# Whole PSUM banks for the low-rank expansion from tile 80 on, with V on four row tiles

## The chip, the cores and the metric

The kernel runs on one core of a Trainium2 chip. A core has a matrix engine (TensorE, PE in the profile), VectorE (DVE), ScalarE (ACT), GpSimd (POOL) and SyncE (SP). Each takes its own instructions in order, and semaphores join them. Matmuls write to PSUM, which is cut into 8 banks of 512 fp32 columns on 128 partitions. DVE and ACT move results from there to SBUF. The metric is the device time of one execution in microseconds (us); the median of three runs is 323.24 (323.01 to 324.3).

## The reference

There are 8 batches of 4224 positions with 192 channels. First comes a short causal convolution along the positions: 7 taps, one softmaxed set of taps for each of 8 heads of 24 channels. Then comes a mixer, whose low-rank part mixes positions (U and V have rank 32), and whose second part is a two-layer network on the channels (192 to 768 to 192).

```python
x = conv(x, softmax(weight))              # (8, 4224, 192), called y in the kernel
h = x.transpose(0, 2, 1) @ U @ V          # U: 4224 x 32, V: 32 x 4224
u = x + h.transpose(0, 2, 1)
out = u + np.maximum(u @ w_ch1, 0.0) @ w_ch2
```

## The kernel before

The positions of a batch are cut into 33 tiles of 128, so that there are 264 tiles in all. Eight tiles make a group, and there are 33 groups. A batch's 33 tiles and a group's 8 don't divide each other, so a group can hold tiles of two batches.

For each batch the steps are these. `conv32` (c) makes y: eight matmuls a head (L349), written to two banks that `evac` copies to SBUF on ACT (L266) or DVE (L268). A string of letters, used in a ring, says which engine takes which copy. It reads x and a shifted copy of x, which POOL makes in six copies (`x_shift`, L303 to L315); there is one such buffer, so the shift for the next batch starts after the conv of this one. `tt_mm` (t) multiplies the 33 tiles by U (L412, four column tiles of the array at a time), `tt_split` makes a high and a low bf16 part (L426 on ACT, L427 on DVE), and `tt_sum` (s) adds the four column tiles with two matmuls (L438), so that the product of rank 32 then stands four times, on partitions 0, 32, 64 and 96; DVE copies it to SBUF (L432).

For the tiles of a batch `h_tiles` (h) expands that product by V: one matmul a tile (L469) with 32 rows, 128 output partitions and 192 columns. The four places of 32 rows in the array, here called row tiles, can work side by side. Two neighbouring tiles form a pair. A pair shares a bank (384 of the 512 columns) and a row tile, the pair's number modulo four, and V is stored in `V_sb` for each tile on that row tile alone. One DVE instruction (L492) adds y and writes a pair's u in bf16; where a pair is cut by the edge of a batch, of a half group or of the span, there are two. When a group's u is whole, SP issues a DMA transpose of it (`transp`, L513).

For each group `w1` runs 36 matmuls (L589), in pairs on two row halves, 512 columns each; a pair of banks is emptied by ACT and DVE with a relu (L603, L605). `w2` runs 12 matmuls (L616) for two tiles, DVE adds u (L625), and SP issues the DMA to the output (L633).

The schedule is written out by hand. `SLOTS` is a list of stages. From stage 5 on a stage runs w1 of three groups (108 matmuls of L589), and then 12 w2 pieces of 12 matmuls. Between the w2 pieces a table says what else PE does at which piece p (0 to 12): c, t, s, h, and x for POOL's shift. Loads of x for later batches are issued by POOL and held back until a certain matmul of w1 is done (`LOADS`). PSUM has one pool of eight banks; each `bank()` takes the next in turn, and waits until that bank's last reader is done. The h spans of the late stages are in `spans`, two or three in a stage:

```python
        5: [(80, 88), (88, 96), (96, 105)],
        6: [(105, 117), (117, 129)],
```

A `w` entry runs `h_span` over its tiles and then issues the transposes of the groups that it completes. Stage 5 begins with group 6, stage 13 with group 30; the last conv is in stage 9, the last h in stage 12.

Of the kernel before, what the change touches and what calls it, by code (L numbers as in the profile page):

```python
# [7 lines left out]
ALU = mybir.AluOpType  # L8
ACT = mybir.ActivationFunctionType
BF16 = mybir.dt.bfloat16  # L10
# [4 lines left out]
def kernel(  # L15
# [10 lines left out]
    nc = tc.nc  # L26
    P = nc.NUM_PARTITIONS
    B, S, D = x.shape
# [16 lines left out]
    cst = ctx.enter_context(tc.tile_pool(name="cst", bufs=1))  # L45
# [10 lines left out]
    def bank():  # L56
        return psp.tile([P, 512], F32, name="ps", tag="ps")
# [5 lines left out]
    yt = [None] * B  # L63
# [39 lines left out]
    def iota(t, pattern, base, mul):  # L103
# [20 lines left out]
        out=Ur[:, 0:nfull, :], in_=U4[0 : nfull * P, :].rearrange("(k p) c -> p k c", p=P)  # L124
# [29 lines left out]
    for r in range(4):  # L154
        nc.vector.memset(rq[QB * r : QB * r + QB, 0:1], float(QB * r))
    nc.vector.tensor_scalar(
        out=rq[:, 1:2], in0=rq[:, 0:1], scalar1=-4.0, scalar2=None, op0=ALU.mult
# [19 lines left out]
    for hh in range(2):  # L177
# [3 lines left out]
        out=dif[:], in0=dif[:], scalar1=rq[:, 0:1], scalar2=None, op0=ALU.add  # L181
# [5 lines left out]
        out=d_sb[:],  # L187
        in0=w_sb[:],
        in1=mx_sb[:].unsqueeze(2).to_broadcast([P, H, KC]),
        op=ALU.subtract,  # L190
# [5 lines left out]
        out=hot[:],  # L196
        in0=dif[:].unsqueeze(1).to_broadcast([P, KC, BW]),
        in1=tap[:].unsqueeze(2).to_broadcast([P, KC, BW]),
        op=ALU.is_equal,
# [3 lines left out]
        out=ident[:], in0=fp[:], scalar1=float(P), scalar2=None, op0=ALU.is_equal  # L203
# [9 lines left out]
        out=c_sb[:].rearrange("p k h -> p h k"),  # L213
        in0=e_sb[:],
        in1=rs_sb[:].unsqueeze(2).to_broadcast([P, H, KC]),
        op=ALU.mult,
    )
    prs = []
    for hh in range(2):
# [3 lines left out]
            out=pr[:],  # L223
            in0=hot[:].unsqueeze(2).to_broadcast([P, KC, HQ, BW]),
            in1=c_sb[:, :, HQ * hh : HQ * hh + HQ].unsqueeze(3).to_broadcast([P, KC, HQ, BW]),
            op=ALU.mult,
# [5 lines left out]
        out=Eq[:], in0=efp[:], scalar1=rq[:, 1:2], scalar2=None, op0=ALU.is_equal  # L232
# [3 lines left out]
        out=fp[:], in0=fp[:], scalar1=R - 1, scalar2=None, op0=ALU.bitwise_and  # L236
# [3 lines left out]
        out=R4[:], in0=fp[:], scalar1=0.0, scalar2=None, op0=ALU.is_equal  # L240
# [163 lines left out]
    ttb = [[] for _ in range(B)]  # L404
# [17 lines left out]
    def tt_split(b, p):  # L422

        hi = sml.tile([P, D], BF16, name="tt_hi")
        lo = sml.tile([P, D], BF16, name="tt_lo")
        nc.scalar.activation(out=hi[:], in_=p[:, 0:D], func=ACT.Copy)  # L426
        nc.vector.tensor_tensor(out=lo[:], in0=p[:, 0:D], in1=hi[:], op=ALU.subtract)  # L427
        ttb[b] += [hi, lo]
# [22 lines left out]
    def u_group(g):  # L451
        if ut[g] is None:
            ut[g] = us.tile([P, 4, 3, 2, HB], BF16, name="u_sb")
        return ut[g]
# [46 lines left out]
    def h_span(t0, t1):  # L501
        while t0 < t1:
            b = t0 // NT
            te = min(t1, (b + 1) * NT)
            h_tiles(b, t0 - b * NT, te - b * NT)
            t0 = te

    def h_group(g):
        h_span(g * GT, g * GT + GT)

    def transp(g):
        uTt[g] = uts.tile([P, 4, 3, P], BF16, name="uT")
        return nc.sync.dma_start_transpose(  # L513
            out=uTt[g][:].rearrange("p i c t -> p (i c) t"),
            in_=ut[g][:].rearrange("p i c f k -> p (i c f k)"),
        )
# [118 lines left out]
    def held(ins, after):  # L635
        tc.add_manual_dep(
            ins.ins,
            after.ins.name,
            mybir.DependencyInfo(mybir.DependencyClass.Sync, mybir.DependencyReason.DATA),
            reason="transfer held back",  # L640
        )

    def x_load(b, q, after):
        if q == 0:
            x_tile(b)
            x_zero(b, nc.gpsimd)
        held(x_part(b, *XP[q]), after)
# [25 lines left out]
            },  # L673
        ),
    ]
    spans = {
        5: [(80, 88), (88, 96), (96, 105)],
        6: [(105, 117), (117, 129)],
        7: [(129, 140), (140, 152)],
        8: [(152, 164), (164, 175)],  # L680
        9: [(175, 187), (187, 198)],
        10: [(198, 210), (210, 222)],
        11: [(222, 233), (233, 245)],
        12: [(245, 253), (253, 264)],
        13: [],
    }
    for k in range(5, 14):
        gs = list(range(3 * k - 9, 3 * k - 6))
        hs = [f"w{t0}:{t1}" for t0, t1 in spans[k]]
        if k == 5:  # L690
            at = {
                2: ["c3:0:3:AAD"],
                3: ["c3:3:3:AAD"],
                4: ["c3:6:2:A", "x4:4"],
                5: [hs[0]],
                6: ["t3"],
                8: ["s3", hs[1]],
                11: [hs[2]],
            }
        elif k < 10:  # L700
            b = k - 2
            at = {
                0: [f"c{b}:0:2:AAD"],
                2: [f"c{b}:2:3:A"],
                4: [f"c{b}:5:3:AD"] + ([f"x{b + 1}:4"] if b + 1 < B else []),
                5: [hs[0]],
                9: [f"t{b}", hs[1]],
                12: [f"s{b}"],
            }
        elif k < 13:  # L710
            at = {0 if k == 12 else 2: [hs[0]], 5 if k == 12 else 7: [hs[1]]}
        else:
            at = {}
        SLOTS.append((gs, gs, at))

    LOADS = {3: [(4, 1), (4, 4), (5, 1), (5, 4)]}
    for b in range(4, B):
        g = 3 * b - 6
# [26 lines left out]
    for r, (k0, k1) in KP[2].items():  # L745
        j = NB0 // 2 * r + k0
        nc.gpsimd.tensor_copy(
            out=U4_sb[:, o : o + k1 - k0, :, :],
            in_=U_sb[:]
# [8 lines left out]
        out=V_sb[0:32, 2 * (NT // 8), :], in_=moe_V[:, (NT - 1) * P : NT * P]  # L758
# [35 lines left out]
    for r in range(4):  # L794
        q = slice(QB * r, QB * r + QB)
        for hh in range(2):
            nc.gpsimd.tensor_copy(
                out=band2[q, HQ * hh : HQ * hh + HQ, :],
                in_=bands[hh][q, :, HB * (r % 2) : HB * (r % 2) + QB],
            )  # L800

    def do(what):
        if what[0] == "c":
            b, h0, n, engs = what[1:].split(":")
            conv32(int(b), int(h0), int(n), engs)
            return
        if what[0] == "d":
            for h in range(H):
                last = conv(int(what[1:]), h, 1, [0, 1], "AA" if h == 2 else "AD")
            held(transp(3), last)  # L810
            done.append(last)
            return
        if what[0] == "l":
            b, q = (int(v) for v in what[1:].split(":"))
            x_load(b, q, done[-1])
            return
        if what[0] == "x":
            b, n = (int(v) for v in what[1:].split(":"))
            if not steps:
                steps.extend(x_shift(b))  # L820
            for _ in range(n):
                steps.pop(0)()
            return
        if what[0] == "w":
            t0, t1 = (int(v) for v in what[1:].split(":"))
            h_span(t0, t1)
            for g in range(t0 // GT, t1 // GT):
                transp(g)
            return
        n = int(what[1:])  # L830
        if what[0] == "h":
            h_group(n)
            if n > 1 and n != 3:
                transp(n)
        elif what[0] == "t":
            tt_split(n, tt_mm(n, range(NT)))
        else:
            tt_sum(n)

    for gs1, gs2, at in SLOTS:  # L840
        for g in gs1:
            ends = w1(g, RELU0 if g == 1 else RELU)
            for b, blocks in LOADS.items():
                for q, (gb, m) in enumerate(blocks):
                    if gb == g:
                        x_load(b, q, ends[m])
                        if steps:
                            steps.pop(0)()
            if g == 0:
                do("h2")  # L850
        while steps and gs1 != [3]:
            steps.pop(0)()
        npc = 4 * len(gs2)
        for p in range(npc + 1):
            for what in at.get(p, []):
                do(what)
            if p < npc:
                g, k = gs2[p // 4], p % 4
                if g == NG - 1 and k == 3:
                    w2(g, 6, 1)  # L860
                    w2(g, 7, 1)
                else:
                    w2(g, 2 * k, 2)
# [30 lines left out]
```

## Time and profile before

| what | us |
|---|---|
| median of three runs | 323.24 |
| the profiled execution | 323.12 |
| its span, first to last instruction | 321.3 |
| PE busy | 314.9 (98%) |
| DVE busy | 268.7 (84%) |
| ACT busy | 169.5 (53%) |
| POOL busy | 141.6 (44%) |

The page also gives the groups that the change touches: 264 matmuls of h at L469 with 12.0 us in which at least one is under way, 168 adds at L492 with 65.8 us, and 133 adds of w2 at L625 with 69.5 us. Ten groups (80 tiles) are made before tile 80 in the old way, in both kernels.

How to read it: an engine's busy time is the time in which at least one of its instructions is under way. Matmuls overlap, so the durations of single ones add up to more than that. The chain that ended last follows the work back from the end; a stretch of it that is all PE, without gaps, means that nothing but PE's own instructions set the time there. A wait in a row of another engine costs time only if that engine's work is on this chain.

### The profile page before, as it was taken

The numbers are of one execution on the slowest core, as the hardware profiler recorded it, in microseconds if no ns is written. First come the engines' busy times: TensorE is split into PE (matmuls) and PEld (weight loads), VectorE is DVE, ScalarE is ACT, GpSimd is POOL, SyncE is SP. The second block draws the span as 40 slices with busy tenths as digits, with TensorE's granted clock in tenths as the row PEclk, the third lists the DMA queues.
The fourth block names the chain that finished last, engine by engine and source line by source line (L and its number), as shares of the span: only waits on it lengthen the run. The fifth ranks groups of instructions, "written<-read, shape, count | busy, mean of one in ns | idle before, by whom it ended". The sixth has DMA issues, their size and how long they took to land.

```text
span 321.3 us, 9597 instructions
## 1 busy us (share of the span) xinstructions
PE 314.9 (98%) x4004; PEld 218.7 (68%) x4004; DVE 268.7 (84%) x550; ACT 169.5 (53%) x344; POOL 141.6 (44%) x108
## 2 busy tenths in 40 slices
PE   7999999999999999999999999999999999999996
PEld 3757576478677647946864884686597497487495
DVE  6779989987977986996998699699898888897864
ACT  1766723960874396088249609824904903912910
POOL 8763199529947982993798398000000000000000
PEclk9999999999999999999999999999999999999999
DMA  9999993998997999799799963169077079059035
GB/s 105 191 195 169 196 232 101 196 190 253 210 165 147 263 153 194 189 201 154 191 241 139 191 185 111 52 179 218 2 215 228 3 169 275 2 171 272 2 109 188
DMA packets 122443, 53.39 MB, mean 166 GB/s; under 512 B 87712, under 2 KB 122400, under 8 KB 122400
## 3 DMA queue, kind: packets, MB, share of 16 engines
q1 hardware_dynamic: 84528, 38.08, 46.0%
q0 software_dynamic: 37728, 14.60, 39.6%
q8 instruction: 31, 0.51, 0.7%
q14 instruction: 12, 0.10, 0.1%
q10 hardware_dynamic: 144, 0.10, 0.1%
HBM read 29.22 MB, written 25.95 MB: 172 GB/s over the span
## 4 chain that ended last, share of the span: by engine, by line
PE 91%; ACT 3%; DMA 2%; DVE 2%; POOL 1%; issue 1%; POOLq 0%
PE ps L616 42%; PE ps L589 39%; PE ps L349 3%; PE ps L469 3%; DMA x_sb<-in_x_dram 2%; PE ps L412 2%; ACT rl_sb L603 2%; ACT y_sb L266 1%; PE ps L379 1%; POOL x_sb L79 1%; DVE u_sb L492 1%; DVE rl_sb L605 1%; PE ps L438 0%; PE ps L536 0%; DVE out_sb L625 0%
## 5 line engine op out<-in xcount | busy, mean ns | idle before, releaser
L603 ACT ACTIVATE rl_sb<-ps 128x512 bf16<-128x512 f32 x233 | 124.3, 604 | 89.1 <-PE ps L589 77.6
L616 PE MATMUL ps<-W_sb,rl_sb 128*128 128x192 bf16 x1584 | 139.8, 246 | 0.2
L616 PEld LDWEIGHTS <-rl_sb 128*128 128x128 bf16 x1584 | 128.4, 98 | 12.2 <-issue 11.9
L589 PE MATMUL ps<-uT,W_sb 64*128 64x512 bf16 x1188 | 131.5, 376 | 0.3 <-DVE uT L268 0.2
L605 DVE TENSOR_SCALAR rl_sb<-ps 128x512 bf16<-128x512 f32 x163 | 105.7, 688 | 15.2 <-PE ps L589 14.9
L589 PEld LDWEIGHTS <-W_sb 64*128 64x128 bf16 x1188 | 61.3, 94 | 65.9 <-issue 3.0
L625 DVE TENSOR_TENSOR out_sb<-ps,u_sb 128x384 f32<-128x384 f32 (+1 forms) x133 | 69.5, 550 | 25.9 <-PE ps L616 25.0
L315 POOL COPY xb_sb<-x_sb 32x3072 bf16<-32x3072 bf16 (+1 forms) x24 | 67.7, 2820 | 1.1
L492 DVE TENSOR_TENSOR u_sb<-y_sb,ps 128x192 bf16<-128x192 bf16 (+1 forms) x168 | 65.8, 461 | 0.0
L303 POOL COPY xb_sb<-x_sb 128x3072 bf16<-128x3072 bf16 x12 | 32.9, 2742 | 41.5 <-PE ps L349 33.8
L266 ACT ACTIVATE y_sb<-ps 128x408 bf16<-128x408 f32 (+4 forms) x90 | 38.2, 519 | 11.9 <-PE ps L349 9.8
L79 POOL DMA_DIRECT2D x_sb<-in_x_dram x32 | 27.1, 852 | 12.5 <-PE ps L469 7.7
L268 DVE CAST y_sb<-ps 128x408 bf16<-128x408 f32 (+4 forms) x36 | 19.2, 578 | 1.3 <-PE ps L379 1.2
L426 ACT ACTIVATE tt_hi<-ps 128x192 bf16<-128x192 f32 x8 | 2.6, 330 | 27.4 <-PE ps L412 27.4
L469 PE MATMUL ps<-tt_sb,V_sb 32*128 32x192 bf16 x264 | 12.0, 245 | 0.0
L349 PE MATMUL ps<-x_sb,band 64*32 64x384 bf16 x192 | 11.8, 332 | 0.0
L349 PE MATMUL ps<-xb_sb,band 64*32 64x384 bf16 x192 | 11.8, 331 | 0.0
L469 PEld LDWEIGHTS <-V_sb 32*128 32x128 bf16 x264 | 5.8, 92 | 5.7 <-issue 5.5
L379 PE MATMUL ps<-x_sb,band 64*64 64x240 bf16 (+3 forms) x192 | 8.0, 276 | 0.4 <-DMA x_sb<-in_x_dram 0.3
L379 PEld LDWEIGHTS <-band 64*64 64x64 bf16 x192 | 6.0, 106 | 2.2 <-issue 1.5
L349 PEld LDWEIGHTS <-band 64*32 64x32 bf16 x384 | 4.3, 89 | 4.7 <-issue 2.4
L412 PE MATMUL ps<-y_sb,U_sb 128*32 128x192 bf16 x258 | 7.4, 247 | 0.0
(65 smaller groups left out, 66.5 us busy)
## 6 DMA issues: line engine op xcount, KB each, us to landing
out_dram<-out_sb SPq DMA_DIRECT2D x131, 192.0 KB, 3.0
x_sb<-in_x_dram POOLq DMA_DIRECT2D x14, 384.0 KB, 7.2
x_sb<-in_x_dram POOLq DMA_DIRECT2D x7, 432.0 KB, 7.8
x_sb<-in_x_dram POOLq DMA_DIRECT2D x7, 408.0 KB, 7.2
W_sb<-in_moe_w_ch_dram POOLq DMA_DIRECT2D x3, 288.0 KB, 7.5
x_sb<-in_x_dram POOLq DMA_DIRECT2D x1, 504.0 KB, 7.4
uT<-u_sb SPq DMA_TRANSPOSE x31, 3.8
x_sb<-in_x_dram POOLq DMA_DIRECT2D x1, 480.0 KB, 5.6
```

The source lines that it names most:

```text
L79: return nc.gpsimd.dma_start(out=xt[b][HB * r : HB * r + HB, s0:s1, :], in_=x[b, blk * HB : (blk + s1 - s0) * HB, :].rearrange("(j p) d -> ...
L266: nc.scalar.activation(out=out, in_=in_, func=ACT.Copy)
L303: nc.gpsimd.tensor_copy(out=xbt[b][:, s0:s1, :], in_=xt[b][:, s0 + 1 : s1 + 1, :])
L315: nc.gpsimd.tensor_copy(out=xbt[b][q, s0:s1, :], in_=xt[b][q, s0:s1, :])
L349: nc.tensor.matmul(out=pp[r][QB * cg : QB * cg + QB, 0 : nk[r] * GS], lhsT=w[hr], rhs=t[hr, st : st + 2 * nk[r] - 1 : 2, hs], start=True, ...
L469: last = nc.tensor.matmul(out=banks[pr][:, a * D : (a + 1) * D], lhsT=V_sb[32 * q : 32 * q + 32, (j // 8) * 2 + j % 2, :], rhs=ttb[b][32 * ...
L492: nc.vector.tensor_tensor(out=u_group(g)[:, i : i + n, :, hf, :], in0=yt[b][:, run[0] : run[0] + n, :].rearrange("p n (c k) -> p n c k", c=3),
L589: last = nc.tensor.matmul(out=pps[m][hf][:], lhsT=W1_sb[HB * hf : HB * hf + HB, c, m * P : (m + 1) * P], rhs=uTt[g][HB * hf : HB * hf + HB ...
L603: nc.scalar.activation(out=rl[:, m, hf, :], in_=pp[hf][:], func=ACT.Relu)
L605: nc.vector.tensor_scalar_max(out=rl[:, m, hf, :], in0=pp[hf][:], scalar1=0.0)
L616: last = nc.tensor.matmul(out=cps[:, a * D : (a + 1) * D], lhsT=rlt[g][:, m, hf, (i + a) * P : (i + a + 1) * P], rhs=W2_sb[:, m, :], start ...
L625: nc.vector.tensor_tensor(out=o[:, 0:n, :].rearrange("p n (c k) -> p n c k", c=3), in0=cps[:, 0 : n * D].rearrange("p (n c k) -> p n c k", ...
```

## The change

From tile 80 on the columns of u are counted in units of 64 (three to a tile). A bank takes eight units, all of its 512 columns, whatever tiles they belong to; a tile that falls across two banks is done in two matmuls of 64 and 128 columns. So eight tiles fill three banks, with ten matmuls in place of eight. Each bank's matmuls stand on one row tile, and the banks of a cluster take the four row tiles in turn, four banks at a time; within such a four the first matmul of each bank is issued, then the second of each, and so on. For that, any tile may be needed on any row tile, so a second copy of V, whole on each of the four, is loaded by POOL in four DMAs after w1 of group 5 (`V4_sb`). DVE adds y for a whole bank at once, cut where a half group or a batch ends: 96 adds where there were 119.

The tiles 80 to 263 are 69 banks. They are made in 14 clusters of 4, 6 or 7 banks, in place of 17 clusters of 8 to 12 tiles. The tables of the stages 5 to 13 are rewritten, with the convs, the products by U, the sums and the shifts in new places, and with other engines for some copies of y (one copy fewer on DVE in stages 5 and 6, two more in each of 7 to 9). In the strings below, `7:b7` means a cluster of 7 banks ahead of w2 piece 7.

```diff
+    TH0 = 80
+    NCH = 3 * TH0
+    V4_sb = cst.tile([P, NT, P], BF16, name="V4_sb")
+
+    def v4_load():
+        for q in range(4):
+            nc.gpsimd.dma_start(
+                out=V4_sb[32 * q : 32 * q + 32, :, :],
+                in_=moe_V[:, :].rearrange("r (j t) -> r j t", t=P),
+            )
+
+    made = [0]
+
+    def h_banks(n):
+
+        c0 = NCH + 8 * made[0]
+        made[0] += n
+        c1 = c0 + 8 * n
+        assert c1 <= 3 * NTT
+        for s0 in range(c0, c1, 32):
+            ps, todo = [], []
+            for k in range(s0, min(s0 + 32, c1), 8):
+                p, q, parts = bank(), len(ps), []
+                for t in range(k // 3, (k + 7) // 3 + 1):
+                    a, e = max(k, 3 * t), min(k + 8, 3 * t + 3)
+                    parts.append((p, q, k, t, a, e))
+                ps.append((p, k))
+                todo.append(parts)
+            for n in range(max(len(parts) for parts in todo)):
+                for parts in todo:
+                    if n >= len(parts):
+                        continue
+                    p, q, k, t, a, e = parts[n]
+                    nc.tensor.matmul(
+                        out=p[:, HB * (a - k) : HB * (e - k)],
+                        lhsT=V4_sb[32 * q : 32 * q + 32, t % NT, :],
+                        rhs=ttb[t // NT][
+                            32 * q : 32 * q + 32, HB * (a - 3 * t) : HB * (e - 3 * t)
+                        ],
...
+            for p, k in ps:
+                a = k
+                while a < k + 8:
+                    b, blk = a // (3 * NT), a // 12
+                    e = min(k + 8, 12 * (blk + 1), 3 * NT * (b + 1))
...
+                    nc.vector.tensor_tensor(
...
+                    a = e
+        for g in range(c0 // 24, c1 // 24):
+            transp(g)
...
-    spans = {
-        5: [(80, 88), (88, 96), (96, 105)],
-        6: [(105, 117), (117, 129)],
-        7: [(129, 140), (140, 152)],
-        8: [(152, 164), (164, 175)],
-        9: [(175, 187), (187, 198)],
-        10: [(198, 210), (210, 222)],
-        11: [(222, 233), (233, 245)],
-        12: [(245, 253), (253, 264)],
-        13: [],
+    late_slots = {
+        5: "2:c3:0:3:AAD 4:c3:3:3:AAAD 5:c3:6:2:A 5:x4:4 7:b7 7:t3 12:s3",
+        6: "0:b4 2:c4:0:2:A 4:c4:2:3:AD 5:c4:5:3:A 5:x5:4 7:b7",
+        7: "0:c5:0:2:AD 0:t4 0:c5:2:3:AD 2:s4 3:c5:5:3:AAAD 3:x6:4 4:b4 7:b4",
+        8: "0:c6:0:2:AAD 1:c6:2:3:AAD 2:c6:5:3:AD 2:x7:4 2:t5 2:b4 4:s5 7:b6",
+        9: "0:c7:0:2:AD 1:c7:2:3:AAD 5:c7:5:3:AAD 6:b4 9:b4 9:t6 9:t7 12:s6 12:s7",
+        10: "0:b4 6:b6",
+        11: "0:b4 6:b7",
+        12: "0:b4",
+        13: "",
     }
...
-        if k == 5:
-            at = {
-                2: ["c3:0:3:AAD"],
-                3: ["c3:3:3:AAD"],
-                4: ["c3:6:2:A", "x4:4"],
-                5: [hs[0]],
-                6: ["t3"],
-                8: ["s3", hs[1]],
-                11: [hs[2]],
-            }
-        elif k < 10:
-            b = k - 2
-            at = {
-                0: [f"c{b}:0:2:AAD"],
-                2: [f"c{b}:2:3:A"],
-                4: [f"c{b}:5:3:AD"] + ([f"x{b + 1}:4"] if b + 1 < B else []),
-                5: [hs[0]],
-                9: [f"t{b}", hs[1]],
-                12: [f"s{b}"],
-            }
-        elif k < 13:
-            at = {0 if k == 12 else 2: [hs[0]], 5 if k == 12 else 7: [hs[1]]}
-        else:
-            at = {}
+        at = {}
+        for item in late_slots[k].split():
+            p, what = item.split(":", 1)
+            at.setdefault(int(p), []).append(what)
         SLOTS.append((gs, gs, at))
...
-        if what[0] == "w":
-            t0, t1 = (int(v) for v in what[1:].split(":"))
-            h_span(t0, t1)
-            for g in range(t0 // GT, t1 // GT):
-                transp(g)
+        if what[0] == "b":
+            h_banks(int(what[1:]))
             return
...
+            if g == 5:
+                v4_load()
```

More of the change, by code (lines that the diff above doesn't have):

```diff
@@ L506, in h_span @@
             t0 = te
+    TH0 = 80
[33 more added lines that the diff above has]
+                        ],
+                        start=True,
+                        stop=True,
+                        tile_position=(32 * q, 0),
+                    )
+            for p, k in ps:
[3 more added lines that the diff above has]
+                    e = min(k + 8, 12 * (blk + 1), 3 * NT * (b + 1))
+                    y0, i0 = a - 3 * NT * b, a - 12 * blk
+                    nc.vector.tensor_tensor(
+                        out=u_group(blk // 2)[:].rearrange("p i c f k -> p (i c) f k")[
+                            :, i0 : i0 + e - a, blk % 2, :
+                        ],
+                        in0=yt[b][:].rearrange("p j (c k) -> p (j c) k", c=3)[
+                            :, y0 : y0 + e - a, :
+                        ],
+                        in1=p[:, HB * (a - k) : HB * (e - k)].rearrange(
+                            "p (n k) -> p n k", k=HB
+                        ),
+                        op=ALU.add,
+                    )
+                    a = e
+        for g in range(c0 // 24, c1 // 24):
+            transp(g)
@@ L688 @@
         gs = list(range(3 * k - 9, 3 * k - 6))
-        hs = [f"w{t0}:{t1}" for t0, t1 in spans[k]]
-        if k == 5:
-            at = {
-                2: ["c3:0:3:AAD"],
-                3: ["c3:3:3:AAD"],
-                4: ["c3:6:2:A", "x4:4"],
-                5: [hs[0]],
-                6: ["t3"],
-                8: ["s3", hs[1]],
-                11: [hs[2]],
-            }
-        elif k < 10:
-            b = k - 2
-            at = {
-                0: [f"c{b}:0:2:AAD"],
-                2: [f"c{b}:2:3:A"],
-                4: [f"c{b}:5:3:AD"] + ([f"x{b + 1}:4"] if b + 1 < B else []),
-                5: [hs[0]],
-                9: [f"t{b}", hs[1]],
-                12: [f"s{b}"],
-            }
-        elif k < 13:
-            at = {0 if k == 12 else 2: [hs[0]], 5 if k == 12 else 7: [hs[1]]}
-        else:
-            at = {}
+        at = {}
+        for item in late_slots[k].split():
+            p, what = item.split(":", 1)
+            at.setdefault(int(p), []).append(what)
         SLOTS.append((gs, gs, at))
```

## The prediction

> **What bounds the kernel now.** I read the page's busy shares first, then the chain that ended last, then that chain in order of time, and last the timeline of single engines in one late stage.
>
> The page says that TensorE (PE) is busy nearly always, at a granted clock (PEclk) of nine tenths or more of full speed in every slice, and that the chain is made of its work:
>
> ```profile
> span 321.3 us, 9597 instructions
> ...
> PE 314.9 (98%) x4004; PEld 218.7 (68%) x4004; DVE 268.7 (84%) x550; ACT 169.5 (53%) x344; POOL 141.6 (44%) x108
> ...
> PEclk9999999999999999999999999999999999999999
> ...
> PE 91%; ACT 3%; DMA 2%; DVE 2%; POOL 1%; issue 1%; POOLq 0%
> ```
>
> Now one late stage (k = 8) of the chain in order of time; the columns are start, length, what and how many. Some matmul records are missing, so counts of L349 are low (16 and 24 were issued).
>
> ```profile
> 164.42 11.76 PE ps L589 x108
> 176.18 0.47 PE ps L349 x11
> 176.65 2.09 PE ps L616 x24
> 178.74 0.64 PE ps L349 x19
> 179.38 2.08 PE ps L616 x24
> 181.46 0.64 PE ps L349 x19
> 182.10 1.10 PE ps L616 x12
> 183.20 0.43 PE ps L469 x12
> 183.63 4.07 PE ps L616 x48
> 187.70 0.85 PE ps L412 x33
> 188.55 0.51 PE ps L469 x11
> 189.06 3.08 PE ps L616 x36
> 192.14 0.17 PE ps L438 x2
> ```
>
> Each piece starts where the one before it ends: PE is the bound from the first w1 of stage 5 (80.51 us) to the last w2 matmul (318.17), 237.66 us. Only PE's own work there, or a new wait in it, can move the end. Two prices follow. From 12 to 24 matmuls of L616 is 1.10 to 2.09, so a matmul of 192 columns takes 82.5 ns and **each run of one kind costs about 0.11 us beyond its matmuls** (L412: 9 rounds x 0.0825 + 0.11 = 0.85; L469 x12: 4 rounds + 0.10). s (L438) after w2 adds only its two matmuls and opens no run. Second, **an h cluster lasts as long as its fullest row tile**: by the code the 12 tiles at 183.20 put 2, 2, 4, 4 on the four row tiles (4 x 0.0825 = 0.33), the 11 tiles at 188.55 put 5, 2, 2, 2, and last longer. A model of pieces plus 0.11 to 0.13 a run gives 237.7 for the whole stretch, so there are no hidden waits in it to win back.
>
> **The change part by part.**
>
> *h matmuls.* Before, 17 clusters; summing the fullest row tile of each gives 63 rounds x 82.5 ns = 5.20 us. After, 69 banks in 14 clusters (nine of 4 banks, two of 6, three of 7), the k-th bank of every four on row tile k: 19 rounds of 512 columns. Matmuls go from 184 to 230: 138 of 192 columns, 46 of 128, 46 of 64. The durations of 192 columns (82.5 ns), 408 (a conv head, 0.17 us) and 512 (L589: 11.65 us over 54 pairs, 216 ns) lie on one line, 0.417 ns a column and 2.4 ns a matmul. By it 512 columns in three or four pieces take 0.22 us: 19 x 0.22 = 4.25, a **saving of 0.95**. No row shows a 64-column piece. If every piece costs a whole 82.5 ns, a four-piece bank takes 0.33 and the sum is 6.2: a loss of 1.0. If the row tiles keep step (each round as long as its longest piece), 0.267 a round, 5.05: a saving of 0.15. I take the line through the durations, as all rows lie on it, and keep both.
>
> That row tiles do not keep step the windows show, for the matmuls of L469 in the cluster at 188.48 (PE and weight loads that touch each stretch):
>
> ```profile
> 188.47:188.56 0.09, 0.08 (x4) 0.09 (x8) 1.00 1.10 294
> 188.56:188.63 0.07, 0.07 (x8) 0.07 (x9) 1.00 1.02 326
> ```
>
> Four matmuls run in the first 0.09 us, though in program order the second of them stands on the same row tile as the first and must wait 82 ns. The others passed it. The Trainium skill ("TensorE: Matmul & The Clock Gate", Part 3, "What overlaps and what doesn't") says that matmuls start and end strictly in program order; by it the sum would be the 5.05 above, and the trace disagrees with it here.
>
> *Fewer runs on PE.* Counting the runs of one kind in program order, s with w2: before 16 in stage 5, 12 in each of 6 to 9, 6, 6, 5, 2 = 83; after 11, 11, 11, 11, 12, 5, 5, 3, 2 = 71. They go because clusters are fewer, a tt or an h stands straight behind a conv or an h, and t6 and t7 stand together. 12 x 0.11 = **1.3 saved** (1.2 to 1.6 with conv's 0.13). w1, w2, conv, tt and s keep their matmuls: nothing.
>
> *PSUM banks.* A cluster of 7 takes seven of the eight; the w2 piece behind it gets the bank of the w2 just before it. That one's add starts 0.03 us after its matmuls and takes 0.56 (the L625 row), so the bank is free after 0.65, while the cluster lasts 0.11 + 0.44: a **wait of about 0.1, three times**. Behind 6 banks or 4 the next bank has been free for 1 us. All this holds if VectorE (DVE) is in step when the cluster starts, as it is before the clusters of today:
>
> ```profile
> 180.51 0.56 DVE L625 TENSOR_TENSOR out_sb<-ps,u_sb 128x384 f32<-128x384 f32 x1 [1.18 <-PE ps L616]
> 181.50 0.56 DVE L625 TENSOR_TENSOR out_sb<-ps,u_sb 128x384 f32<-128x384 f32 x1 [0.43 <-PE ps L616]
> ```
>
> *DVE.* 119 adds (65 of 384 columns, 54 of 192) become 96 (44 of 512, 44 of 256, 8 others) over the same columns; by 547 and 347 ns a fixed 147 ns is saved 23 times at most. Four more y copies (0.55 each) go from ACT to DVE. Stages 6, 8, 10 and 11 get 3 to 6 more tiles (0.25 us each by L492's 5.6 us for 23) and 7 to 9 two more copies, so at most 1.5 us on 23.7 to 24.2 busy of some 27.8 (in 10 and 11 on 22 of 24.9). All off PE's path. Behind a 7-bank cluster DVE holds some 4.4 us of adds; PE runs on, as it asks for one bank per 1.0 us and DVE frees one per 0.6 to 0.7. What is queued behind them, the w2 adds and then the first relu of w1, is under a microsecond late, and each group of w1 leaves DVE 0.6 idle (its waits in L605) to catch up.
>
> *POOL and its DMAs.* The four V loads (0.5 to 1 us to issue each, by the V_sb and x rows) fall in POOL's idle stretch before 70.66 (6.2 us, it waits there for conv). They move 1.1 MB in bf16; by queue q0's 14.6 MB for 39.6% of the span that is some 9 us of the 16 engines, first used near 99 us. Without that cover the first cluster would wait. On SP only transposes move; each group is written at least 6 us before its w1, against 3.8 us to land. In stage 6 the shift of x for batch 5 (L303 to L315) starts one w2 piece later and conv 5 opens stage 7. POOL needs 19.4 us from release to the last copy:
>
> ```profile
> 126.63 2.74 POOL L303 COPY xb_sb<-x_sb 128x3072 bf16<-128x3072 bf16 x1 [7.05 <-PE ps L349]
> ...
> 142.94 3.06 POOL L315 COPY xb_sb<-x_sb 32x3456 bf16<-32x3456 bf16 x1
> ```
>
> PE arrives after 2.09 + 0.55 + 5.06 + 11.76 = 19.5 (today 21.9). With 0.1 to start, a **wait of 0.1**, where it was covered by 2.4. The other stages keep 2 us or more.
>
> *Sum.* 0.95 + 1.3 - 0.4 = 1.85 us. The profiled execution took 323.12 (321.3 and 1.8 around the span), 0.12 below the median of 323.24; from the median: **321.4 us**.
>
> **The rivals.** A measurement of this kernel can tell 0.5% (1.6 us) from no change: the bounds are 321.6 and 324.9.
>
> 1. *Short pieces cost a whole slot.* For: 46 more matmuls, each with its own weight load, 0.09 us by the PEld row. Against: on the row tile with five tiles, pieces follow each other every 82 ns, so a load is hidden behind 80 ns of work; for 27 ns of work nothing shows it. h then costs 6.2: 323.3 us. The Trainium skill (same page and part) lets a weight load overlap only matmuls on other row groups, which is this rival's mechanism.
> 2. *Row tiles in step.* Against it stand the windows above: 322.2 us.
> 3. *DVE empties the banks too late (slower).* Everything a large cluster writes is emptied by DVE alone. If DVE is 0.7 us or more behind when such a cluster starts, the next w2 waits for that long each time, and a late bank goes on into w1. Five large clusters at 0.7 eat the gain and give 324.9; at 1.0 each, 326. For: DVE already has 85% in these stages, and more y copies in 7 to 9. Against: the idle 0.43 before its w2 adds. At the far end, all of a cluster's adds ahead of the next w2 (4.4 us), the times would be near 340, but the order of the banks excludes it.
>
> **How the numbers follow.** The forecast has 0.56 and a range of its own of 320.4 to 322.2 (no new waits and 0.13 a run; pieces at 50 ns): 0.45 below 321.6, 0.11 above. Rival 1 has 0.12, rival 2 0.10, both within 0.5%; rival 3 has 0.22. So faster 0.45, same 0.33, slower 0.22. The likeliest is 321.4; the range 320.4 to 324.9 leaves out most of rival 3 and a little below.
>
> **What would show it.** In the chain in order of time: a 4-bank cluster of 13 or 14 matmuls at 0.33 us (0.44 for rival 1, 0.38 for rival 2), a 7-bank one at 0.55; 71 runs between 80.5 us and the end. PE waiting for DVE behind the large clusters for more than 0.1 us would be rival 3; a gap before the first conv of stage 7 with POOL as its releaser is the late shift. DVE's wait rows for PE before w2 adds should shrink but not vanish. I am wrong if PE's pieces no longer follow each other without gaps, or if a run costs less where it stands behind another kind than w2.

## The result, and the profile after

| | before | after |
|---|---|---|
| median, us | 323.15 (323.01 to 324.3) | 332.64 (332.01 to 337.57) |
| the profiled execution, us | 323.12 | 332.01 |
| its span, us | 321.3 | 330.2 |

The change made the kernel slower, by a ratio of 1.0279 (1.0242 to 1.0316). The forecast was 321.4. Ratios here and below are made from undisturbed executions alone, so some are lower than the medians beside them would give.

The page of the kernel after still has PE busy nearly always, but for one dent, and there the granted clock falls too:

```profile
PE   8999999995499999999999999999999999999996
...
PEclk9999999999599999999999999999999999999999
...
PE 88%; DMA 6%; DVE 2%; ACT 2%; issue 1%; POOL 0%; DVEq 0%; POOLq 0%
```

The 40 slices are 8.3 us each; the dent is in the tenth and eleventh, 74 to 91 us. It is in stage 4, before the first of the new clusters. The chain in order of time shows what stands there (start, length, what, how many):

```profile
73.39 1.92 PE ps L681 x22
75.31 11.00 DMA out_dram<-out_sb
...
86.42 0.43 DVE u_sb L492 x2
...
87.54 0.47 PE ps L469 x5
88.02 2.06 PE ps L681 x12
90.08 12.85 PE ps L654 x108
```

The same place in the chain of the kernel before:

```profile
80.51 11.84 PE ps L589 x108
92.34 2.09 PE ps L616 x24
```

The first w1 of stage 5 (that of group 6) now begins at 90.08, 9.57 late. It takes 12.85 where it took 11.84, because the clock is still 0.50 after the pause. By the end of this w1 10.59 us are lost. From there to the last w2 matmul it is 224.11 (102.93 to 327.04) where it was 225.83 (92.34 to 318.17): **1.72 gained**. So the profiled execution is 8.9 us longer: 10.59 lost in one place, 1.72 won in the rest.

Of the 9.57, 7.5 is time in which PE does nothing, from 79.07 to 86.56. The rest is lost in the matmuls behind it, which wait for DVE to catch up and run at the lower clock: 12 matmuls of w2 take 2.06 (88.02) where they took 1.10.

The waits say who stopped whom. PE waits for DVE to make banks free (and stands before an old cluster, L469); DVE waits for an output buffer, which is free when the output from it has landed (us in all, times, the longest):

```profile
DVE out_sb L690 <- DMA out_dram<-out_sb: 9.6, 1, 9.6
...
PE ps L469 <- DVE out_sb L690: 7.5, 1, 7.5
```

The outputs are issued by SP. Its timeline before, and then after (start, duration, what):

```profile
66.67 2.50 SPq L513 DMA_TRANSPOSE uT<-u_sb  x1
69.26 8.71 SPq L633 DMA_DIRECT2D out_dram<-out_sb  x9
79.24 1.41 SPq L513 DMA_TRANSPOSE uT<-u_sb  x1
```

```profile
66.61 7.61 SPq L578 DMA_TRANSPOSE uT<-u_sb  x1
74.31 12.59 SPq L698 DMA_DIRECT2D out_dram<-out_sb  x9
88.44 1.41 SPq L578 DMA_TRANSPOSE uT<-u_sb  x1
```

A transpose whose issue took 2.50 now holds SP for 7.61. It lands after 19 us, the longest of uT's landings, which go from 7.9 to 19.0 (a landing is counted from the issue; before, then after):

```profile
DMA to landing us min/median/max: 3.2/3.8/7.9
```

```profile
DMA to landing us min/median/max: 3.2/3.5/19.0
```

The windows show the transfers at this moment (length, then PE, PEld, DVE, ACT, POOL, clock, share of the 16 DMA engines, GB/s): first before, then after.

```profile
74.00:78.00 4.00, 4.00 (x54) 3.69 (x52) 2.86 (x8) 0.00 (x0) 3.96 (x2) 1.00 1.10 366
78.00:82.00 4.00, 4.00 (x50) 2.70 (x49) 4.00 (x10) 0.66 (x2) 3.88 (x3) 1.00 0.89 176
```

```profile
74.00:78.00 4.00, 4.00 (x54) 3.69 (x53) 1.52 (x4) 0.00 (x0) 3.96 (x2) 1.00 1.33 142
78.00:82.00 4.00, 1.07 (x13) 0.93 (x12) 0.00 (x0) 0.00 (x0) 3.88 (x3) 1.00 1.31 22
```

At 78 to 82 us packets are under way on the DMA engines for more of the time than before (the share, a sum over the queues that can pass 1, is 1.31 against 0.89), and yet only 22 GB/s are moved, where it was 176. What is new among the transfers is the load of V, which POOL issues in 2.03 us right before, as forecast, and which takes 16.1 us to land:

```profile
64.38 2.03 POOL L514 DMA_DIRECT2D V_sb<-in_moe_V_dram  x4
```

```profile
V_sb<-in_moe_V_dram POOLq DMA_DIRECT2D x4, 264.0 KB, 16.1
```

The DMA queues of the kernel after from 78 to 82 us (packets, MB, share of the 16 engines' time) show why so little moves. q0 is POOL's queue, q1 SP's:

```profile
q1 hardware_dynamic: 144, 0.04, 125.1%
q0 software_dynamic: 9, 0.05, 6.1%
```

The load's queue takes 6.1% of 16 engines, which is the time of one. The packet records have one row of 8448 bytes after another there, 0.64 us each, the last of them until 82.9. In the same 4 us SP's queue starts only 144 packets of 256 bytes, and they take a median of 0.66 us where 0.02 is usual. From 83 to 87 us, with the last row gone, 347 GB/s are moved. So the end of the load, on what looks like a single engine (the records name none), held back transfers that are spread over all of them.

### The profile page after: what moved, and what is told of

The parts are those of the page before. It is cut to its first block, busy times and chain, and to the rows that moved or that the text cites. A ratio compares the mean times of both kernels' runs of the same rounds, so it can differ in the third digit from the quotient of the medians.

```text
span 330.2 us, 9677 instructions
## 1 busy us (share of the span) xinstructions
PE 316.9 (96%) x4050; PEld 218.4 (66%) x4050; DVE 269.9 (82%) x531; ACT 167.8 (51%) x340; POOL 143.6 (43%) x112
## 4 chain that ended last, share of the span: by engine, by line
PE 88%; DMA 6%; DVE 2%; ACT 2%; issue 1%; POOL 0%; DVEq 0%; POOLq 0%
PE ps L681 40%; PE ps L654 39%; DMA out_dram<-out_sb 3%; PE ps L349 3%; DMA x_sb<-in_x_dram 2%; PE ps L412 2%; PE ps L379 2%; PE ps L541 1%; ACT rl_sb L668 1%; DVE u_sb L492 1%; DVE out_sb L690 1%; PE ps L469 1%; ACT y_sb L266 1%; DVE rl_sb L670 1%; PE ps L601 0%
## 5 line engine op out<-in xcount | busy, mean ns | idle before, releaser
L681 PEld LDWEIGHTS <-rl_sb 128*128 128x128 bf16 x1584 | 129.7, 98 | 10.0 <-issue 8.2
L654 PEld LDWEIGHTS <-W_sb 64*128 64x128 bf16 x1188 | 58.8, 94 | 69.6 <-issue 4.6
L266 ACT ACTIVATE y_sb<-ps 128x384 bf16<-128x384 f32 (+4 forms) x86 | 36.4, 519 | 17.0 <-PE ps L349 15.1
L557 DVE TENSOR_TENSOR u_sb<-y_sb,ps 128x512 bf16<-128x512 bf16 (+5 forms) x96 | 44.1, 527 | 0.0
L268 DVE CAST y_sb<-ps 128x408 bf16<-128x408 f32 (+4 forms) x40 | 21.3, 577 | 1.3 <-PE ps L379 1.2
L492 DVE TENSOR_TENSOR u_sb<-y_sb,ps 128x384 bf16<-128x384 bf16 (+1 forms) x49 | 19.9, 471 | 0.0
L469 PE MATMUL ps<-tt_sb,V_sb 32*128 32x192 bf16 x80 | 4.8, 255 | 7.7 <-DVE out_sb L690 7.5
L469 PEld LDWEIGHTS <-V_sb 32*128 32x128 bf16 x80 | 1.9, 92 | 10.9 <-issue 10.9
L163 PE MATMUL ps<-zz 128*128 128x512 f32 (+1 forms) x10 | 7.2, 878 | 1.1 <-DVE zz L151 1.1
L426 ACT ACTIVATE tt_hi<-ps 128x192 bf16<-128x192 f32 x8 | 2.6, 330 | 10.2 <-PE ps L412 10.2
## 6 DMA issues: line engine op xcount, KB each, us to landing
V_sb<-in_moe_V_dram POOLq DMA_DIRECT2D x4, 264.0 KB, 16.1
```

Of the source, the lines that this page charges most:

```text
L266: nc.scalar.activation(out=out, in_=in_, func=ACT.Copy)
L492: nc.vector.tensor_tensor(out=u_group(g)[:, i : i + n, :, hf, :], in0=yt[b][:, run[0] : run[0] + n, :].rearrange("p n (c k) -> p n c k", c=3),
L557: nc.vector.tensor_tensor(out=u_group(blk // 2)[:].rearrange("p i c f k -> p (i c) f k")[:, i0 : i0 + e - a, blk % 2, :], in0=yt[b][:].rea ...
L654: last = nc.tensor.matmul(out=pps[m][hf][:], lhsT=W1_sb[HB * hf : HB * hf + HB, c, m * P : (m + 1) * P], rhs=uTt[g][HB * hf : HB * hf + HB ...
L681: last = nc.tensor.matmul(out=cps[:, a * D : (a + 1) * D], lhsT=rlt[g][:, m, hf, (i + a) * P : (i + a + 1) * P], rhs=W2_sb[:, m, :], start ...
```

## The experiments

The first theory (A) is that the load of V alone costs the time, and that the rest of the change does what the prediction summed. The rival (B) is that the banked clusters or the new places of the work lose time too. Within A it was open how the load does it: by the length of its rows, by its amount, or by its place on a queue.

**The load alone (e1).** The kernel before, with V4_sb loaded and not used:

```diff
+            if g == 5:
+                v4_load()
```

> The kernel before, with the four loads of V added after w1 of group 5 and their data used by nothing. Theory A (the load holds up the transpose of group 7 and the outputs behind it on SP's queue; PE then stands still and its clock drops): 332 to 335 us, 323.15 plus the whole 9.6 us that stage 4 lost and some 1 us of lower clock, with DVE waiting 9 to 10 us for an output's landing near 76 us. Rival B (the late stages lose the time: banks, DVE, POOL): 323 us.

Measured: 333.41 (329.08, 331.37, 335.45 and 337.77), ratio 1.0199 (1.0146 to 1.0252). That is 5.7 to 14.4 us over the kernel before, and the mean granted clock is 0.98 to 0.99 in all four, against 1.00 before. In the profiled execution, the longest of them, the wait of DVE for an output is there (9.5 us), SP is held for 11.37 us by the transpose, and a landing of uT takes 20.5; 3.0 us more are a pause of PE that the profile gives no releaser for. So the load alone makes a loss of this kind and size, and nothing of the clusters is needed for it. Its size differs too much from one execution to the next to say from e1 that it is the whole of the loss; that takes the next run.

**The rest alone (e6).** The change without the load: POOL fills V4_sb with zeros, so h from tile 80 on is left out of the result, while every instruction of PE, DVE, ACT and SP stays.

```diff
+    nc.gpsimd.memzero(V4_sb[:])
...
-            if g == 5:
-                v4_load()
```

> The changed kernel without the load of V4: POOL fills V4_sb with zeros at the start instead, so h from tile 80 on is zero and that part of the result is left out; every instruction on PE, DVE, ACT and SP stays. Theory A (the whole loss is the load's, and the sum of the prediction holds for the rest): 321.3, between 321.0 and 321.8; w1 of group 6 starts at 80.5. Theory B (the banked clusters lose time too, in stage 4 or late): 325 or more.

Measured: 321.62 (321.52 to 323.3), ratio 0.9941 (0.992 to 0.9963): 2.0 us under the 323.59 of the kernel before in the same runs. The rest of the change loses nothing, so B falls. (The profiled execution, 323.3, has a pause of 1.55 us on PE at 75.4 that the profile gives no releaser for; the other five lie between 321.52 and 321.99.)

**Shorter rows (e2, e5).** V4_sb laid out so that a row of V comes in 11 pieces of 768 bytes, not in one of 8448. The tile's second size is `3 * P + 8` in e2 and `3 * P + 32` in e5:

```diff
-    V4_sb = cst.tile([P, NT, P], BF16, name="V4_sb")
+    V4_sb = cst.tile([P, 11, 3 * P + 32], BF16, name="V4_sb")
...
-                in_=moe_V[:, :].rearrange("r (j t) -> r j t", t=P),
+                in_=moe_V[:, :].rearrange("r (j t) -> r j t", t=3 * P),
```

> The changed kernel, V stored with a gap of 16 bytes behind every three tiles, so that a row moves as 11 pieces of 768 bytes and not as one of 8448. Theory A1 (the length of the packets does the harm: one of 642 ns is put between the short ones of the transpose): 320.9 to 322.5 us, no wait of DVE for outputs near 76 us. Theory A2 (the same bytes on the queue at that moment do it, whatever the packets): 330 to 335. Rival B: 332, as nothing of the late stages is touched.

> The changed kernel with V4_sb laid out in 11 pieces of 768 bytes a row with 64 bytes of gap between them, so that every later tile keeps an offset that is a multiple of 64 bytes; the same 1.1 MB at the same place. e2 had the same pieces with a gap of 16 bytes and was 328.9. Theory A1 (the long rows of 8448 bytes hold up the transposes): w1 of group 6 starts within 1 us of before's 80.51 and the time is 321.3 to 322.5. Theory A2 (the amount at that moment is what holds them up, however it is cut): w1 of group 6 starts 5 to 10 us late, 328 to 335. If A1 falls and w1 of group 3 is on time, where e2 had it 2.7 us late, the shifted tiles had a price of their own.

Measured: 328.92 (327.91 to 330.06) and 328.59 (328.14 to 330.29). w1 of group 6 is 7.1 and 5.7 us late. A1 falls; A2's range holds the time of e5, and that of e2 lies between the two ranges. The long rows are some 4 us of the loss at most; most of it stays when they are gone. The queues of e5 show both parts, from 74 to 78 us and then from 83 to 86:

```profile
q0 software_dynamic: 789, 0.55, 90.1%
q1 hardware_dynamic: 788, 0.20, 38.6%
```

```profile
q1 hardware_dynamic: 1422, 1.03, 103.3%
q0 software_dynamic: 55, 0.03, 7.5%
```

First the two queues move packet for packet, 789 and 788, so the load still takes its turns among the transposes and outputs. Then the load's last pieces again take about one engine's time (7.5%), but in pieces of 0.08 us they no longer hold the others up: 354 GB/s are moved. In e2 w1 of group 3 was 2.7 late already, in e5 0.3; but the median landing of uT is 4.4 in both, against 3.5 after, so the new sizes did something to the transposes that these two runs don't explain.

**More output buffers (e3).**

```diff
-    outs = ctx.enter_context(tc.tile_pool(name="outs", bufs=8))
+    outs = ctx.enter_context(tc.tile_pool(name="outs", bufs=13))
```

> The changed kernel with 13 output buffers in place of 8: the load and its packets stay as they are. If PE stood still because DVE had no free output buffer (the last link of theory A), DVE goes on, and the transpose that lands at 83 us is still in time for its w1 at 84: 321.3 to 323.5 us. If the transpose itself was what PE waited for, or rival B: 331 to 333.

Measured: 335.08 (330.75 to 336.06), ratio 1.0304 (1.0229 to 1.038). DVE's wait for outputs is gone, w1 of group 6 begins at 80.38, and then w1 of group 8 waits for its transpose. The chain in order of time:

```profile
79.28 1.10 PE ps L681 x12
80.38 4.73 PE ps L654 x43
85.11 9.88 DMA uT<-u_sb
...
95.03 6.65 PE ps L654 x36
```

So the buffers are only the first to run out. Behind them stands the transpose itself; more buffers move the pause from one wait to another.

**Outputs on another queue (e12).** In e3 and in the kernel after, the outputs of stage 4 stand behind a late transpose on SP's queue. Here ACT issues them on its own.

```diff
-        eng = nc.scalar if t + n == NTT else nc.sync
+        eng = nc.scalar if t + n == NTT or 3 <= g < 6 else nc.sync
```

> The changed kernel, load of V4 included, with the outputs of groups 3 to 5 (stage 4) issued by ACT on its own queue, so that they no longer stand behind the transposes of groups 6 to 8 on SP's. Theory Q (the outputs are late because the transpose ahead of them on SP's queue is): DVE no longer waits for outputs by 5 us or more, w1 of group 6 starts within 2 us of 80.5; what is left is a wait for a late transpose as in e3 (w1 of group 7 or 8 late by up to 7): 326 to 331. Theory E (the 16 engines are taken by the load's packets, and outputs wait whatever their queue): DVE still waits 5 us or more for outputs, w1 of group 6 is 6 to 10 us late: 330 to 334.

Measured: 330.75 in two executions (329.27 and 332.24). w1 of group 6 is 7.5 late, as theory E has it, but not by the wait that E named: DVE no longer waits for an output, which was a sign of Q. The outputs are slow on a queue with no transpose in it: the list of DMA issues from 66 to 84 us gives them a median of 14.6 us to land (4.7 in the same stretch of the kernel before). ACT itself is held for 5.70 us while it issues one; the split of t (L426) stands behind that on ACT, and PE waits for it. The chain and the waits show it:

```profile
out_dram<-out_sb ACTq DMA_DIRECT2D x7, 192.0 KB, 14.6
V_sb<-in_moe_V_dram POOLq DMA_DIRECT2D x1, 264.0 KB, 16.8
uT<-u_sb SPq DMA_TRANSPOSE x1, 20.1
```

```profile
74.21 5.70 ACTq L698
```

```profile
PE ps L438 <- ACT tt_hi L426: 3.8, 1, 3.8
```

So the order on SP's queue is not what makes the outputs late. While the load is under way, transposes and outputs are late whichever queue they are on. The Trainium skill ("DMA: Bandwidth & Descriptors", "Issuing engines are not separate DMA queues") says that DMAs run on the same 16 DMA engines and interleave there, whichever engine issued them; the 14.6 us of e12 agree with it.

**Half of it (e10).** Two row tiles of V4 by DMA at the same place; POOL copies the other two from `V_sb`, inside SBUF, behind the loads of x for batch 4 (the copies are those of e9, below).

```diff
     def v4_load():
-        for q in range(4):
+        for q in range(2):
...
+            if g == 7:
+                v4_copy(2)
+                v4_copy(3)
```

> The changed kernel with half of the load: two of the four row tiles of V4 come by DMA at the same place, the other two by POOL's copies from V_sb behind the loads of x for batch 4. Theory P (the transposes and outputs of stage 4 are late by the time that the load takes, less a fixed cover): half of the load, some 2.6 us of the 16 engines less, leaves w1 of group 6 3 to 6 us late, 324 to 327.5. Theory C (the cover of 6 us between a transpose and its w1 takes half a load): on time, 321.3 to 322.3.

Measured: 329.0 (327.07 to 331.0), ratio 1.017 (1.0132 to 1.0209). w1 of group 6 begins at 85.97, 5.5 late. Theory C, that a cover of 6 us takes half a load, falls. With 9.6 late for the whole load and on time for none (e9), a half costs 5.5: about in proportion, with no cover, each by one profiled execution. P's lateness came; the median is above the time that P expected.

**Other places (e4, e7, e8).** The load after the shift copies for batch 3 (some 82 us); in one piece near 51 us; and in four, near 48, 51, 55 and 58 us. The diffs are entries in the table of the stages:

```diff
-                4: ["c2:6:2:A", "x3:4"],
+                4: ["c2:6:2:A", "x3:4", "v"],
```

```diff
-            {0: ["d1", "x2:1", "l2:3", "x2:5", "h1"], 1: ["t1"], 3: ["s1"], 4: ["h4"]},
+            {0: ["d1", "x2:1", "l2:3", "x2:3", "v", "x2:2", "h1"], 1: ["t1"], 3: ["s1"], 4: ["h4"]},
```

```diff
+            {0: ["d1", "x2:1", "l2:3", "x2:2", "v0", "x2:1", "v1", "x2:1", "v2", "x2:1", "v3", "h1"], 1: ["t1"], 3: ["s1"], 4: ["h4"]},
```

> The changed kernel with the four loads issued behind POOL's copies of x for batch 3 in stage 4, near 82 us in place of 64: same packets, but the transpose of group 7 and the outputs of stage 4 are through by then. Theory A: 321 to 323 us (what it can still hold up are the transpose of group 9 and the first outputs of stage 5, which have 8 us and more to spare). If the amount of data in all was too much for the queues: 328 to 333, the wait in another place.

> The changed kernel with the four loads of V4 issued by POOL between two of its shift copies for batch 2, near 51 us, where before's transfers take the least of the 16 engines (0.13 to 0.29). Theory A (the load hurts only where transposes and outputs that are due stand behind it): w1 of group 6 on time, 321.3 to 322.5; what is at risk is the transpose of group 5, wanted near 59.7: at worst 3 us more. Theory A3 (1.1 MB costs its some 9 us wherever it stands): 328 or more.

> The changed kernel with the four loads of V4 apart from each other, each behind one of POOL's shift copies for batch 2 (near 48, 51, 55 and 58 us). Theory A (a queue of long rows is what holds the transposes up; a quarter of it holds them up a quarter as long, about 2 us, which the 6 us between a transpose and its w1 cover): 321.3 to 322.5. Theory A3 (the load costs its time wherever it stands): 328 or more.

Measured: e4 332.63 as the median of ten that run from 322.03 to 337.2 (five above 333), with a ratio of 1.0033 (0.9988 to 1.0078); e7 327.03 (326.83 to 327.88); e8 326.93 (325.18 to 329.27). In e4's profiled execution (325.49) the output waits are gone, w1 of group 6 is on time, and w1 of stage 7 waits for a transpose that was issued at 132, long after the load. The trace shows a way from one to the other: the loads of x for batch 4 stand behind V's on POOL's queue and take 15.6 to 20 us to land, POOL's shift then waits 10.1 us for them, and from 104 to 110 us, when two transposes are due, POOL's queue still takes 64.7% of the engines' time, where in e9 it moves nothing. These two hold SP for 8.82 us, against 3.25, and the next loads of x are issued 4.7 us later than in e9 (116.44 against 111.72). No run tests that way. Why its executions differ so much stays open. In e7 the load lands in 5.4 us, and still w1 of group 5 waits for its transpose, as its chain shows; stage 5 then starts 6.5 late:

```profile
54.57 8.78 DMA uT<-u_sb
...
63.40 6.37 PE ps L654 x30
```

In e8 w1 of group 5 is 1.0 late and that of group 6 3.2. So in the profiled executions the load had a cost at each of these places. The stretch near 51 us, taken for quiet by its share of the engines (0.13 to 0.29, and 0.87 from 50 to 52 us), is one where the next transpose is wanted 5 us after its issue.

**No transfer at all (e9).** V is already in SBUF, a quarter on each row tile. POOL copies the other three quarters to each row tile; a tile's own quarter is read where it is.

```diff
-    def v4_load():
...
+    def v4_copy(q):
+        for s in range(4):
+            if s == q:
+                continue
+            nc.gpsimd.tensor_copy(
+                out=V4_sb[32 * q : 32 * q + 32, 0 : NT - 1, :].rearrange(
+                    "p (k s a) t -> p k s (a t)", s=4, a=2
+                )[:, :, s, :],
+                in_=V_sb[32 * s : 32 * s + 32, 0 : 2 * (NT // 8), :].rearrange(
+                    "p (k a) t -> p k (a t)", a=2
+                ),
+            )
...
-            if g == 5:
-                v4_load()
+            if g in (5, 7):
+                v4_copy(g - 5)
+                v4_copy(g - 4)
```

> The changed kernel with V4 made without any DMA: POOL copies it inside SBUF from the V_sb that is already there, 12 copies of 32x1024 and three of 32x128 (a row tile's own quarter is read from V_sb), half of them behind the loads of x for batch 3 and half behind those for batch 4. By the rows of POOL's copies (32x3456 in 3.06 us) a copy takes about 0.95, 6 us a half, in idle stretches of 6.2 and 8.8 us in which POOL waits for conv. Theory A (only the transfer did harm; the rest of the change gains what the prediction summed): 321.3 to 321.9, 0.5 to 0.7% faster than before, w1 of group 6 at 80.5. Theory D (POOL's copies get into DVE's way, or the shift of x comes late): 322.5 or more, with a wait for POOL in front of conv.

Measured: **321.43** (321.33 to 321.79) against 323.42 in the same runs, ratio 0.9935 (0.992 to 0.9949). This is the version that beats both kernels, by 2.0 us and 11. A copy takes 1033 ns, not 950, and the first half runs into the shift of x by 0.9 us, which costs nothing: POOL's timeline has no idle time in between, and PE's pieces in stage 4 follow each other as before.

```profile
64.86 4.25 POOL L516 COPY V_sb<-V_sb 32x1024 bf16<-32x1024 bf16 x4
69.06 0.29 POOL L525 COPY V_sb<-V_sb 32x128 bf16<-32x128 bf16 x1
69.39 2.11 POOL L516 COPY V_sb<-V_sb 32x1024 bf16<-32x1024 bf16 x2
71.56 2.74 POOL L303 COPY xb_sb<-x_sb 128x3072 bf16<-128x3072 bf16 x1
```

**The price of the short pieces (e11).** e9 with all banks on row tile 0, so that the 230 matmuls follow each other there:

```diff
-                p, q, parts = bank(), len(ps), []
+                p, q, parts = bank(), 0, []
```

> The kernel with V copied by POOL, with every bank of every cluster on row tile 0 instead of on four in turn, so that all 230 matmuls of h from tile 80 on follow each other on one row tile; V4 is copied for that row tile alone. The order of the work stays. It measures the two disputed prices of the prediction with much leverage. Forecast's line (a piece costs its columns, 0.417 ns each and 2.4 ns): 69 banks of 0.221 are 15.3 us instead of 4.25, less some 0.3 of bank waits behind the clusters of 7, which then last longer: +10.7 on 321.4, 332.1; a cluster of 4 banks takes 0.99. Rival 1 (a piece costs a whole slot of 82.5 ns, its weight load not hidden): 230 x 82.5 ns = 19.0, +14.5, 335.9; a cluster of 4 takes 1.2. If the four row tiles gave nothing (all in program order): no change, 321.4.

Measured: 332.16 (331.92 to 332.77), against 332.1 by the line and 335.9 by rival 1. In the chain a cluster of 4 banks takes 0.99, one of 7 takes 1.65:

```profile
101.54 1.65 PE ps L557 x23
...
121.02 0.99 PE ps L557 x14
```

Four banks in a row are 4 x 0.22 + 0.11 = 0.99. A piece of 64 columns costs its columns, and its weight load is hidden even when all stand on one row tile.

## Why the prediction was wrong, point by point

**The step that failed is "POOL and its DMAs".** It costed the four loads at nothing: they "fall in POOL's idle stretch before 70.66" and are "first used near 99 us. Without that cover the first cluster would wait." Both hold near enough (POOL issued them from 64.38 to 66.4, and in e9 the first cluster stands at 101.7), and neither was the point. The step asked when the load is issued and when its own data are wanted. It did not ask who else wants the 16 DMA engines while it is under way. From 66 us on these were the transpose and the outputs of stage 4, and the same step let them pass with "on SP only transposes move" and "3.8 us to land", a median over the whole run. The sum covers only the stretch from 80.51 us on, as if nothing that the load does before it could move the end; the wait came before it, at 79 us. In place of nothing the load cost 10.59 us in the profiled execution: w1 of group 6 began 9.57 late, 7.5 of that with PE doing nothing, and took 1.01 more at the lower clock. The trace of before had the warning: the engines' share is 1.60 from 66 to 70 us, the loads of x for batch 3, and the longest landing of a transpose was 7.9. Half a load is not covered either (e10).

**No rival had it.** The one on the slower side was about DVE and PSUM banks. Its kind of chain came (DVE late, PE waits for a bank), but the releaser was an output's landing, in a stage before the new clusters.

**The rest of the sum was right.** 1.85 was forecast for it; the profiled execution gained 1.72 behind the loss, e6 was 2.0 below before, e9 2.0, at 321.43 where 321.4 was forecast. Its terms:

- *h matmuls*: clusters of 4 banks take 0.33, one of 6 banks 0.55, as the chain of e9 has them, between pieces without gaps. Rival 2 would have 0.38, rival 1 0.44. e11 prices a bank at 0.22, on the line, so the weight loads are hidden there too.

```profile
154.26 0.33 PE ps L557 x10
154.58 3.08 PE ps L697 x36
157.66 0.34 PE ps L557 x10
158.00 5.06 PE ps L697 x60
...
185.23 0.55 PE ps L557 x16
```

- *Fewer runs on PE*: not measured by a run of its own; a run's 0.11 is in the 0.99 and 1.65 of e11, and the sum comes out with it. That a run costs the same behind another kind than w2 the chain of e9 shows at the start of stage 7, where a t stands straight behind a conv and a conv behind it: 0.85 and 0.64, as elsewhere.
- *PSUM banks*: behind a cluster of 7 the chain of e9 goes through DVE, and from the end of the w2 before it to the next piece of PE it is 0.63, against 0.55 for the cluster: 0.08, where 0.1 was forecast.

```profile
99.72 2.10 PE ps L697 x24
101.82 0.02 issue
101.84 0.57 DVE out_sb L706
...
102.45 0.90 PE ps L412 x33
```

- *DVE*: rival 3 didn't come. The waits of PE for DVE behind large clusters stay at that 0.1.
- *POOL's shift in stage 7*: forecast 0.1, none seen. The first conv there follows w1 directly (147.30 in e9, right at the end of the w1 from 135.54).

## What to carry to other kernels

A transfer has two prices: when its data are wanted, and whom it delays while it is under way. So look up the share of the DMA engines at the moment of issue, and then the slack of every transfer that is due in the next ten or so microseconds (here a transpose and the outputs behind eight buffers), by its own landing time there and not by a median. Data that are already in SBUF can be copied by an engine that idles: some 13 us of POOL's time in place of 1.1 MB of DMA turned a loss of 9.5 us into a gain of 2.

## What the runs showed of the hardware

- A load of 1.1 MB in rows of 8448 bytes, some 16 us from issue to landing beside the loads of x, lengthened a transpose's landing from at most 7.9 to 19 us, and outputs on a queue of their own stood at a median of 14.6 (e12). Cut in pieces of 768 bytes it still held up w1 of group 6 by 5.7 us (e5). The Trainium skill ("DMA: Bandwidth & Descriptors", "Queues, rings and completion order") says that an engine takes its queues in turn and finishes a whole packet of one before the next. By that rule long packets hold up the small ones of a transpose, and shorter ones hold them up less: 9.6 against 5.7 us of delay agrees in direction, and so do the 789 and 788 packets of e5. The order on a single engine no run here shows, as the records name no engine.
- The tail of a load can hold up the rest: while rows of 8448 bytes still took the time of one engine in 16 (after, 78 to 82 us), all transfers together moved 22 GB/s; with pieces of 768 bytes in the same place (e5, 83 to 86 us) 354.
- The queue of an engine that issues DMAs can hold the engine itself: SP 7.61 us for one transpose, ACT 5.70 for one output.
- PE stood from 79.07 to 86.56 us. By windows of 1 us the granted clock was 1.00 until 82, 0.50 from 83 on, and 0.87 from 92 to 93; 12 matmuls of w2 took 2.06 in place of 1.10, and a w1 12.85 in place of 11.84.
- Matmuls of 64, 128 and 192 columns behind each other on one row tile cost their columns (0.22 us for 512), with a weight load for each.
